# Attention work in pairs: scores and a quarter of M issued one behind the other, over four PSUM banks, from the third batch on

## The chip, the cores and the metric

One Trainium2 chip, one of its cores. The metric is the device time of one execution in microseconds (us), the median of three runs. TensorE is PE in the profile, with its weight loads apart as PEld; VectorE is DVE, ScalarE is ACT, SyncE, which issues all DMAs here, is SP.

## The reference

```python
def sm_attn(qq, kk, vv):                       # 8 batches, 8 heads, 576 tokens, head size 64
    s = scale * np.matmul(qq, kk.transpose(0, 1, 3, 2))
    s = s - np.max(s, axis=-1, keepdims=True)
    a = np.exp(s)
    a = a / (np.sum(a, axis=-1, keepdims=True) + 1e-09)
    return np.matmul(a, vv)
p_packed = sm_attn(p, k, v)                    # 32 landmarks p per head
out = sm_attn(q, p_packed, p_packed)
x = out as (4608, 512)
h = np.maximum(x @ w_in, 0.0); x = h * h @ w_out            # first MLP, 2048 wide
h = x @ w_in2; g = h / (1.0 + np.exp(-1.702 * h)); g @ w_out2   # second MLP, 2048 wide
```

All in fp32.

## The kernel before

**Stages.** The first half of the span holds the attention and the first MLP, the second half the second MLP (`mm_a`, `mm_b`), which the change leaves alone. In the first part the work goes by *slots*: one slot is one chunk of 128 of the 2048 hidden columns for one half (288 tokens) of one batch. Slots 0 to 63 serve batches 0 and 1; from then on every batch has 32 slots, two halves of 16. A slot issues on PE six matmuls `h` (`mm1`, recorded at L112, the helper `prod`) and twelve matmuls `y` (`mm2`, L524). ACT takes `h` out of PSUM with a relu (L493) and squares it (L503; three chunks of 16 are squared on DVE, L501), ACT and DVE split the square into two parts (L202, L204), and `y` reads these. `h` runs three slots ahead of `y` (`LA = 3`, L37).

**Attention beside it.** x is never formed with `w_in`: M = (second softmax's values) times `w_in` is built in four quarters of 512 columns (`m_step`, L450 to L472), and `h` multiplies M by the softmax weights `a`. The attention of batch b runs in the 32 slots of batch b-1, at slots that the list `steps` (L874 to L877) gives, counted from s0 = 32(b-1): scores of the landmarks with k, one half of the tokens each (`s1`, L309) at 0 and 1; their exponentials (`s1b`) at 4; transposes and products with v (`tr`, `pv`, `t2`) at 7 to 10; scores of q, one half each (`s2a`, L394) at 12 and 17, with their softmax (`s2b`) at 16 and 20 and split (`s2c`) at 17 and 26; the quarters of M (`m_step`) at 19, 21, 26 and 29.

**PE's part of these.** `s1`, `s2a` and `m_step` all issue 16 small fp32 matmuls through `heads` (L299 to L307): for each of eight heads, 64 rows by 32 columns of the array, so that the eight occupy it side by side, and each in two instructions. The other work on PE uses the full 128 by 128 array. Two result tiles take two PSUM banks.

**PSUM.** Eight banks: four for `y` (`acc`), two for `h` (`mm_p`), two for attention (`at_p`). `att_tile` (L294) gives an attention tile a bank of `at_p`, and one of `mm_p` only in batch 0. Results leave so: M by two ACT copies (L468) and two DVE subtractions (L470), q scores by two DVE transposes (L401), landmark scores of the first half by a DVE maximum (L319) and an ACT copy (L323) each, of the second half by a maximum and, at `s1b`, the exponentials (L338).

**Order.** Every engine runs its own queue in program order. One pass of the loop at L1000 issues the splits of the slot two ahead, the `h` of the slot three ahead, the `y` of its own slot, and then what `plan[s]` lists, step by step in turn (`interleave`, L811). Conversions of the second MLP's weights (L145 to L155, L230 to L251) are listed in the same plan, about two every eight slots of those whose number modulo 16 is 1 to 13 (`CALM`).

**Loads.** A quarter of M reads two tiles of `w_in` (`load_win`, 512 KB each), through three buffers. They are issued at slot 9 (three; for batch 2 at 14) and then two, two and one at the slots of the first, second and third quarter (`ws`, L884 to L889); each waits until the quarter that used the buffer has been computed. All DMAs go through SP's one queue.

Of the kernel before, what the change touches and what calls it, by code (L numbers as in the profile page):

```python
# [8 lines left out]
F32 = mybir.dt.float32  # L9
# [13 lines left out]
P = 128  # L23
# [52 lines left out]
def fused_kernel(ctx, tc, qT, kT, vv, pT, w_in, w_out, w_in2, w_out2, out):  # L76
# [217 lines left out]
    def att_tile(b, alt, name):  # L294

        pool, tag = (mm_p, "mm") if b == 0 and alt else (at_p, "at")
        return pool.tile([P, 512], F32, tag=tag, name=name)
# [11 lines left out]
    def s1(b, hf):  # L309
        c = slice(hf * HS, (hf + 1) * HS)  # L310
        ps = [att_tile(b, hf, f"s1_{b}_{hf}_{r}") for r in range(2)]
# [35 lines left out]
    def tr(b, r):  # L347
# [6 lines left out]
        pa_ = att_tile(b, r, f"tr_{b}_{r}_a")  # L354
        pb_ = att_tile(b, r, f"tr_{b}_{r}_b")
# [14 lines left out]
    def pv(b, r):  # L370
        t = e1T.pop((b, r))
        v = vt.pop((b, r))
        ps = att_tile(b, r, f"pv_{b}_{r}")
        for c in range(5):
            n = P if c < 4 else 64
            for hp in range(4):
                nc.tensor.matmul(ps[32 * hp:32 * hp + 32, :D], t[:n, c, 32 * hp:32 * hp + 32], v[:n, c, hp * D:(hp + 1) * D],  # L377
                                 start=c == 0, stop=c == 4)
        yield 1
        if r == 0:  # L380
            pp[b] = pp_p.tile([P, 2, D], F32, tag="ppb", name=f"ppb{b}", bufs=1)
        nc.vector.tensor_scalar(out=pp[b][:, r, :], in0=ps[:, :D], scalar1=rs[b][:, 5, r:r + 1], scalar2=None, op0=ALU.mult)
# [11 lines left out]
    def s2a(b, hf):  # L394
        ps = [att_tile(b, hf == 0, f"s2_{b}_{hf}_{r}") for r in range(2)]
# [54 lines left out]
    def m_step(b, f):  # L450
        w = [wt.pop((b, f, g)) for g in range(2)]
        if (b, f) == (0, 0):
            ps = [acc_p.tile([P, 512], F32, tag=f"acc{r}", name=f"m_{b}_{f}_{r}") for r in range(2)]
        else:
            ps = [at_p.tile([P, 512], F32, tag="at", name=f"m_{b}_{f}_{r}") for r in range(2)]
# [406 lines left out]

    for b in range(1, B):
# [7 lines left out]
        else:  # L871
            s0 = (b - 1) * 2 * NFC
            at_k, at_v, at_q, at_w = -5, -2, (2, 3, 5, 6), 9
            steps = [(0, s1, 0), (1, s1, 1), (4, s1b), (7, tr, 0), (8, pv, 0), (8, tr, 1), (9, pv, 1),  # L874
                     (10, t2), (12, s2a, 0), (16, s2b, 0), (17, s2c, 0), (17, s2a, 1), (20, s2b, 1), (26, s2c, 1)]

            steps += [(s, m_step, f) for f, s in enumerate((19, 21, 26, 29))]  # L877
# [3 lines left out]
        if b > 1:  # L881
            for s, f, *a in steps:
                at(s0 + s, f, b, *a)
# [116 lines left out]
    for s in range(done("y"), len(slots)):  # L1000
# [9 lines left out]
        drain(second, s)  # L1010
# [32 lines left out]
```

## Time and profile before

| | before |
|---|---|
| three runs | 1433.84 us median, 1433.5 to 1436.06 |
| the profiled execution | 1436.79 us |
| its span | 1434.9 us |
| PE busy | 1412.7 us (98%) |
| ACT busy, DVE busy | 835.8 us (58%), 951.2 us (66%) |
| granted TensorE clock, mean | 0.999 |

The span is what the profiler saw from the first to the last instruction. A busy time counts an engine as busy while any instruction is in flight; matmuls are pipelined, so that a plain slot's six and twelve matmuls last 295 ns and more each but follow each other much more closely. What a group of matmuls costs is therefore read from the start of the group to the start of the next.

### The profile page before, as it was taken

To read this page: it belongs to the slowest core of one execution; us is meant where nothing else is said; L and a number is where in the kernel's file an instruction comes from. 1 tells how busy PE (TensorE), PEld (TensorE's weight loads), DVE (VectorE), ACT (ScalarE), POOL (GpSimd) and SP (SyncE) were. 2 spreads that over 40 slices of the span, in tenths; PEclk is the share of its full clock that TensorE was granted. 3 is DMA by queue.
4 is the path that set the end of the run, shared out by engine and by line. 5 is a ranking of instruction groups with operands and counts; after the bars stand their busy time and mean duration, and the time that the engine had idled before them with its cause. 6 is when DMAs were issued, how large, how long until landed. Compare 5 with 4: busy or idle time off the path is not lost.

```text
span 1434.9 us, 24896 instructions
## 1 busy us (share of the span) xinstructions
PE 1412.7 (98%) x9734; PEld 1262.1 (88%) x9734; DVE 951.2 (66%) x1623; ACT 835.8 (58%) x1740; POOL 0.7 (0%) x6
## 2 busy tenths in 40 slices
PE   6999999999999999999999999999999999999999
PEld 4688989889898998999998888888888888999998
DVE  6896475756757657573255778577855875677585
ACT  5878676676776677765564544454444534544452
POOL 0000000000000000000000000000000000000000
PEclk9999999999999999999999999999999999999999
DMA  9848467576664756541325566656665676688675
GB/s 327 288 148 307 162 207 227 176 235 212 200 229 176 251 182 221 186 149 33 125 99 206 205 244 221 217 206 227 227 227 205 220 250 229 248 300 286 253 293 180
DMA packets 110934, 307.95 MB, mean 215 GB/s; under 512 B 9056, under 2 KB 52192, under 8 KB 96736
## 3 DMA queue, kind: packets, MB, share of 16 engines
q1 hardware_dynamic: 110816, 306.35, 62.1%
q8 instruction: 77, 1.26, 0.4%
q14 instruction: 41, 0.34, 0.1%
HBM read 250.94 MB, written 55.38 MB: 213 GB/s over the span
## 4 chain that ended last, share of the span: by engine, by line
PE 93%; DMA 3%; ACT 3%; DVE 1%; issue 0%; SPq 0%; DVEq 0%; ACTq 0%
PE h L112 37%; PE y L524 27%; PE o L112 24%; PE m L307 2%; PE s L307 1%; PE pv L377 1%; DMA wA<-w_d 1%; PE tr_a L357 1%; DMA win<-win_d 0%; DMA raw_wo<-in_w_out 0%; PE h L486 0%; DMA w_d<-wc 0%; DMA p<-in_pT 0%; PE warm L830 0%; ACT e L338 0%; ACT gh L202 0%
## 5 line engine op out<-in xcount | busy, mean ns | idle before, releaser
L524 PE MATMUL y<-gh,wo 128*128 128x288 f32 x2976 | 434.2, 295 | 0.4 <-ACT gh L202 0.2
L524 PEld LDWEIGHTS y<-gh,wo 128*128 128x128 f32 x2976 | 406.2, 188 | 4.4 <-ACT gh L202 1.3
L112 PE MATMUL h<-y,wA 128*128 128x512 f32 (+1 forms) x1680 | 349.8, 367 | 1.4 <-DMA wA<-w_d 1.4
L112 PE MATMUL o<-g,wB 128*128 128x512 f32 (+1 forms) x1680 | 349.0, 367 | 0.0
L112 PEld LDWEIGHTS h<-y,wA 128*128 128x128 f32 x1680 | 305.6, 188 | 42.1 <-issue 2.0
L112 PEld LDWEIGHTS o<-g,wB 128*128 128x128 f32 x1680 | 305.6, 188 | 39.6 <-DMA wB<-w_d 0.4
L112 PE MATMUL h<-a,M 128*128 128x288 f32 x1488 | 242.8, 299 | 1.3 <-ACT r L493 1.3
L112 PEld LDWEIGHTS h<-a,M 128*128 128x128 f32 x1488 | 207.7, 188 | 37.0 <-issue 27.7
L636 ACT ACTIVATE g<-hid 128x1024 fp32r<-128x1024 f32 (+1 forms) x140 | 132.8, 971 | 131.9 <-DVE hid L631 102.3
L204 DVE TENSOR_TENSOR gh<-gf,gh 128x288 fp32r<-128x288 f32 x248 | 111.6, 452 | 121.4 <-ACT gh L202 121.1
L612 DVE TENSOR_TENSOR g<-hid,g 128x1024 fp32r<-128x1024 f32 (+1 forms) x140 | 152.6, 1113 | 42.3 <-ACT g L636 40.7
L493 ACT ACTIVATE r<-h 128x288 f32<-128x288 f32 x256 | 104.1, 407 | 84.2 <-PE h L112 81.0
L700 ACT ACTIVATE r<-h 128x512 f32<-128x512 f32 (+1 forms) x120 | 66.6, 555 | 118.3 <-PE h L112 116.1
L708 DVE TENSOR_TENSOR hid<-h,r 128x512 f32<-128x512 f32 (+1 forms) x120 | 76.0, 634 | 81.7 <-PE h L112 65.3
L202 ACT ACTIVATE gh<-gf 128x288 fp32r<-128x288 f32 x248 | 108.6, 438 | 5.2 <-DVE gf L501 2.7
L718 DVE TENSOR_TENSOR hid<-hid,sg 128x512 f32<-128x512 f32 (+1 forms) x120 | 75.7, 631 | 47.1 <-ACT sg L714 47.0
L503 ACT ACTIVATE gf<-r 128x288 f32<-128x288 f32 x212 | 94.3, 445 | 6.6
L714 ACT ACTIVATE sg<-hid 128x512 f32<-128x512 f32 (+1 forms) x120 | 70.2, 585 | 30.5 <-DVE hid L708 30.3
L470 DVE TENSOR_TENSOR M<-m,M 128x512 fp32r<-128x512 f32 x62 | 41.9, 688 | 45.9 <-ACT M L468 45.2
L631 DVE TENSOR_TENSOR hid<-hid 128x1024 f32<-128x1024 f32 (+1 forms) x60 | 66.1, 1111 | 0.0
L468 ACT ACTIVATE M<-m 128x512 fp32r<-128x512 f32 x62 | 36.0, 593 | 39.8 <-PE m L307 39.7
L714 ACT ACTIVATE sg<-h 128x512 f32<-128x512 f32 (+1 forms) x40 | 22.3, 557 | 32.7 <-PE h L112 32.7
(110 smaller groups left out, 974.5 us busy)
## 6 DMA issues: line engine op xcount, KB each, us to landing
wB<-w_d SPq DMA_DIRECT2D x70, 1024.0 KB, 5.0
wA<-w_d SPq DMA_DIRECT2D x40, 1024.0 KB, 4.9
wA<-w_d SPq DMA_DIRECT2D x40, 768.0 KB, 6.2
win<-win_d SPq DMA_DIRECT2D x56, 512.0 KB, 5.1
w_d<-wc SPq DMA_DIRECT2D x112, 256.0 KB, 3.4
k<-in_kT SPq DMA_DIRECT2D x32, 288.0 KB, 5.4
y_d<-ysb SPq DMA_DIRECT2D x16, 576.0 KB, 3.8
v<-in_vv SPq DMA_DIRECT2D x16, 512.0 KB, 7.0
```

The source lines that it names most:

```text
L112: nc.tensor.matmul(ps, w, x, start=start and i == 0, stop=stop and i == n - 1, skip_group_check=more)
L202: nc.scalar.activation(hi, x, AF.Copy)
L204: nc.vector.tensor_tensor(out=lo, in0=x, in1=hi.bitcast(F32), op=ALU.subtract)
L493: nc.scalar.activation(r, ps[:, :HS], AF.Relu)
L503: nc.scalar.activation(g, r, AF.Square)
L524: nc.tensor.matmul(accs[d][:, :HS], w[:, d * P:(d + 1) * P], t[:, x_, :], start=first, stop=fc == seg[1] and d not in {o[0] for o in ops[n ...
L612: nc.vector.tensor_tensor(out=t[:, :, 1, :n], in0=src, in1=t[:, :, 0, :n].bitcast(F32), op=ALU.subtract)
L636: nc.scalar.activation(t[:, :, 0, :PAIRS[p]], gop[p, i, g, "src"], AF.Copy)
L700: nc.scalar.activation(t[:, 0, :n], bank[p, c, "1"][:, :n], AF.Copy)
L708: nc.vector.tensor_tensor(out=hid(p, c, blk), in0=bank[p, c, b][:, :n], in1=part[p, c, r][:, 0, :n], op=ALU.add)
L714: nc.scalar.activation(t, bank[p, c, "1"][:, :n] if blk == 2 else hid(p, c, blk), AF.Sigmoid, scale=GELU)
L718: nc.vector.tensor_tensor(out=hid(p, c, blk), in0=bank[p, c, "1"][:, :n] if blk == 2 else hid(p, c, blk), in1=part.pop((p, c, "sg", blk)), ...
```

## The change

`att_tile` now goes by its flag alone, and more tiles take the `mm_p` banks: both halves of the q scores from batch 2 on, the first half of the landmark scores from batch 3 on, and the last quarter of M for batches 2 to 6. The list of steps changes from batch 2 on: each half of the q scores (now at 17 and 22) is followed in the same slot by a quarter of M (the first and the second). The third and fourth quarter of batches 2 to 6 move to slots 32 and 34, which are slots 0 and 2 of the next batch's attention, beside that batch's two halves of the landmark scores (whose second half moves from 1 to 2, and `s1b` from 4 to 5). Batch 7 keeps its last two quarters at 26 and 29. In the slot behind such a joint slot, `y` is issued ahead of the splits and the `h`. These are 12 pairs with q scores (batches 2 to 7) and 10 with landmark scores (batches 3 to 7, beside M of batches 2 to 6).

```diff
@@ -293,7 +293,7 @@
 
     def att_tile(b, alt, name):
 
-        pool, tag = (mm_p, "mm") if b == 0 and alt else (at_p, "at")
+        pool, tag = (mm_p, "mm") if alt else (at_p, "at")
         return pool.tile([P, 512], F32, tag=tag, name=name)
 
     def heads(ps, w, x):
@@ -308,7 +308,7 @@
 
     def s1(b, hf):
         c = slice(hf * HS, (hf + 1) * HS)
-        ps = [att_tile(b, hf, f"s1_{b}_{hf}_{r}") for r in range(2)]
+        ps = [att_tile(b, hf == (0 if b > 2 else 1) and b != 1 and b != 2, f"s1_{b}_{hf}_{r}") for r in range(2)]
         heads(ps, lambda hp: pt[b][:, hp, :], lambda hp: kt[b, hp][:, c])
         if hf == 0:
             rs[b] = st_p.tile([P, 6, 2], F32, tag="st", name=f"st{b}")
@@ -351,8 +351,8 @@
         else:
             t = e1t_p.tile([P, 5 * P], F32, tag="e1t", name=f"e1t_{b}_{r}")
         t = e1T[b, r] = t.rearrange("p (c k) -> p c k", c=5)
-        pa_ = att_tile(b, r, f"tr_{b}_{r}_a")
-        pb_ = att_tile(b, r, f"tr_{b}_{r}_b")
+        pa_ = att_tile(b, b == 0 and r, f"tr_{b}_{r}_a")
+        pb_ = att_tile(b, b == 0 and r, f"tr_{b}_{r}_b")
         for c in range(4):
             nc.tensor.transpose(pa_[:, c * P:(c + 1) * P], e[:, c * P:(c + 1) * P], ident)
         nc.tensor.transpose(pb_[:64, :P], e[:, 512:576], ident)
@@ -370,7 +370,7 @@
     def pv(b, r):
         t = e1T.pop((b, r))
         v = vt.pop((b, r))
-        ps = att_tile(b, r, f"pv_{b}_{r}")
+        ps = att_tile(b, b == 0 and r, f"pv_{b}_{r}")
         for c in range(5):
             n = P if c < 4 else 64
             for hp in range(4):
@@ -392,7 +392,7 @@
     NB = HS // 32
 
     def s2a(b, hf):
-        ps = [att_tile(b, hf == 0, f"s2_{b}_{hf}_{r}") for r in range(2)]
+        ps = [att_tile(b, b > 1 or b == 0 and hf == 0, f"s2_{b}_{hf}_{r}") for r in range(2)]
         heads(ps, lambda hp: ppT[b][:, 32 * hp:32 * hp + 32], lambda hp: qt[b, hp][:, hf * HS:(hf + 1) * HS])
         yield 1
         t = s2_p.tile([P, 2 * NB, 32], F32, tag="s2t", name=f"s2t{b}_{hf}", bufs=1)
@@ -452,7 +452,7 @@
         if (b, f) == (0, 0):
             ps = [acc_p.tile([P, 512], F32, tag=f"acc{r}", name=f"m_{b}_{f}_{r}") for r in range(2)]
         else:
-            ps = [at_p.tile([P, 512], F32, tag="at", name=f"m_{b}_{f}_{r}") for r in range(2)]
+            ps = [att_tile(b, 1 < b < B - 1 and f == 3, f"m_{b}_{f}_{r}") for r in range(2)]
         heads(ps, lambda hp: ppT[b][:, 32 * hp:32 * hp + 32], lambda hp: w[hp // 2][:, hp % 2, :])
         yield 1
         if b == 0 and 4 * f < NFULL:
@@ -860,6 +860,7 @@
         g = running[k] if k in running and name != "warm" else macros[name](*map(int, a))
         running[k] = None if g is None or next(g, running) is running else g
 
+    joint = set()
     for b in range(1, B):
         if b == 1:
             s0 = 0
@@ -871,16 +872,17 @@
         else:
             s0 = (b - 1) * 2 * NFC
             at_k, at_v, at_q, at_w = -5, -2, (2, 3, 5, 6), 9
-            steps = [(0, s1, 0), (1, s1, 1), (4, s1b), (7, tr, 0), (8, pv, 0), (8, tr, 1), (9, pv, 1),
-                     (10, t2), (12, s2a, 0), (16, s2b, 0), (17, s2c, 0), (17, s2a, 1), (20, s2b, 1), (26, s2c, 1)]
-
-            steps += [(s, m_step, f) for f, s in enumerate((19, 21, 26, 29))]
+            s1s = [(0, s1, 0), (1, s1, 1), (4, s1b)] if b == 2 else [(0, s1, 0), (2, s1, 1), (5, s1b)]
+            steps = s1s + [(7, tr, 0), (8, pv, 0), (8, tr, 1), (9, pv, 1), (10, t2), (17, s2a, 0), (17, m_step, 0), (19, s2b, 0),
+                           (21, s2c, 0), (22, s2a, 1), (22, m_step, 1), (25, s2b, 1), (27, s2c, 1)]
+            steps += [(s, m_step, f) for f, s in ((2, 32), (3, 34))] if b < B - 1 else [(26, m_step, 2), (29, m_step, 3)]
+            joint |= {s0 + s for s, f, *a in steps if f is m_step and b < B - 1 or f is s2a}
         ld = loads(b)
         for n, (f, *a) in enumerate(ld):
             at(s0 + (at_k if n < 5 else at_v if n < 7 else at_q[n - 7]), f, *a)
         if b > 1:
             for s, f, *a in steps:
-                at(s0 + s, f, b, *a)
+                (plan[s0 + s].insert(0, (f, (b, *a))) if f is s1 and a == [0] else at(s0 + s, f, b, *a))
         ws = [s for s, f, *_ in steps if f is m_step]
         if b == 2:
             at_w = 14
@@ -997,7 +999,9 @@
     nfirst, nsplit = done("f"), done("g")
     for _ in range(4):
         ahead()
-    for s in range(done("y"), len(slots)):
+
+    def lead(s):
+        nonlocal nfirst, nsplit
         while nsplit < min(s + LA, nfirst):
             drain(parts, nsplit)
             nsplit += 1
@@ -1007,7 +1011,14 @@
         while nsplit <= s:
             drain(parts, nsplit)
             nsplit += 1
-        drain(second, s)
+
+    for s in range(done("y"), len(slots)):
+        if s - 1 in joint and nsplit > s:
+            drain(second, s)
+            lead(s)
+        else:
+            lead(s)
+            drain(second, s)
         interleave(plan[s])
         for _ in range(plan_end[s]):
             ahead()
```

## Rows read from the trace of the kernel before

**Rows 1.** The page: the granted clock in 40 slices.
```profile
PEclk9999999999999999999999999999999999999999
```

**Rows 2.** Windows: length; busy PE, PEld, DVE, ACT, POOL; clock; DMA share; GB/s.
```profile
437.00:513.00 76.00, 76.00 (x642) 69.23 (x641) 51.52 (x117) 54.18 (x141) 0.00 (x0) 1.00 0.60 202
```

**Rows 3.** Timeline of PE, 440 to 460 us: start, time to last end, what.
```profile
448.25 0.95 PE L112 MATMUL h<-a,M 128*128 128x288 f32 x6
449.04 1.74 PE L524 MATMUL y<-gh,wo 128*128 128x288 f32 x12
450.71 0.72 PE L307 MATMUL s<-q,ppT 64*32 64x288 f32 x16
451.36 1.06 PE L112 MATMUL h<-a,M 128*128 128x288 f32 x6
452.25 1.75 PE L524 MATMUL y<-gh,wo 128*128 128x288 f32 x12
...
454.62 1.74 PE L524 MATMUL y<-gh,wo 128*128 128x288 f32 x12
456.30 1.09 PE L307 MATMUL m<-win,ppT 64*32 64x512 f32 x16
457.32 1.06 PE L112 MATMUL h<-a,M 128*128 128x288 f32 x6
458.21 1.75 PE L524 MATMUL y<-gh,wo 128*128 128x288 f32 x12
```

**Rows 4.** Timeline of PE from 19.10 us, cut at 19.40, 19.66 and 19.905.
```profile
19.15 0.48 PE L307 MATMUL s<-q,ppT 64*32 64x288 f32 x8 [0.30 <-ACT ppT L389]
...
19.15 0.91 PE L307 MATMUL s<-q,ppT 64*32 64x288 f32 x17 [0.30 <-ACT ppT L389]
...
19.15 1.15 PE L307 MATMUL s<-q,ppT 64*32 64x288 f32 x23 [0.30 <-ACT ppT L389]
```

**Rows 5.** Timeline, all engines, 276 to 290 us: M's first two quarters, batch 3.
```profile
279.05 1.09 PE L307 MATMUL m<-win,ppT 64*32 64x512 f32 x16
...
280.18 0.88 SPq L290 DMA_DIRECT2D win<-win_d  x2
...
285.01 1.06 PE L307 MATMUL m<-win,ppT 64*32 64x512 f32 x8
...
287.38 1.06 PE L307 MATMUL m<-win,ppT 64*32 64x512 f32 x8 [1.30 <-DMA win<-win_d]
...
288.37 1.06 PE L112 MATMUL h<-a,M 128*128 128x288 f32 x6
```

**Rows 6.** The chain, 455 to 466 us: start, time to the next piece, what.
```profile
462.33 1.40 PE m L307 x16
```

**Rows 7.** L290, the loads of w_in for M, over the whole span.
```profile
DMA to landing us min/median/max: 3.6/5.1/8.1
```

**Rows 8.** Windows, as in rows 2: the stretch that begins with slot 160.
```profile
492.00:494.00 2.00, 2.00 (x27) 1.37 (x26) 1.01 (x3) 0.25 (x1) 0.00 (x0) 1.00 1.01 324
```

**Rows 9.** Timeline, 485 to 489 us: behind a quarter of M (ended at 485.11).
```profile
485.11 1.06 PE L112 MATMUL h<-a,M 128*128 128x288 f32 x6
...
485.27 0.60 ACT L468 ACTIVATE M<-m 128x512 fp32r<-128x512 f32 x1 [1.76 <-PE m L307]
...
487.19 0.58 ACT L468 ACTIVATE M<-m 128x512 fp32r<-128x512 f32 x1
...
487.81 0.69 DVE L470 TENSOR_TENSOR M<-m,M 128x512 fp32r<-128x512 f32 x1 [0.62 <-ACT M L468]
488.01 0.40 ACT L493 ACTIVATE r<-h 128x288 f32<-128x288 f32 x1
```

**Rows 10.** Timeline of ACT, 497 to 503 us: the relu in a slot without attention work.
```profile
499.75 0.41 ACT L493 ACTIVATE r<-h 128x288 f32<-128x288 f32 x1 [0.84 <-PE h L112]
```

**Rows 11.** Timeline of PEld from 19.10 us, cut at 19.41 and 19.42.
```profile
19.14 0.18 PEld L307 LDWEIGHTS s<-q,ppT 64*32 64x32 f32 x16 [0.54 <-ACT ppT L389]
...
19.14 0.38 PEld L307 LDWEIGHTS s<-q,ppT 64*32 64x32 f32 x17 [0.54 <-ACT ppT L389]
```

## The prediction

> **What bounds the kernel now.** The first view is the page: PE is busy 98% of the span and its clock is granted in full in every slice [rows 1], so the clock is no term here. The change touches slots 32 to 223, about a third of the span, and the second view, windows over such a stretch, tells what limits them: in 76 us PE is never idle, ACT is busy 54.18 us and DVE 51.52 us [rows 2]. PE's queue sets the pace, and ACT and DVE have some 30% to spare. A microsecond off PE's queue there is a microsecond off the end, as long as nothing new makes PE wait.
>
> The third view, PE's timeline, tells what a slot costs. Read it from start to start, as the durations overlap. A slot without attention work takes 2.37 us from its `y` to the next (452.25 to 454.62). A slot with a half of the q scores takes 3.21 us (449.04 to 452.25), one with a quarter of M 3.59 us (454.62 to 458.21) [rows 3]. So the half costs **0.84 us** and the quarter **1.22 us**, 2.06 us together. From its first matmul to the `h` behind it the half takes 0.65 us and the quarter 1.02 us [rows 3]; the other 0.19 or 0.20 us is paid at the two edges, where PE goes over to the 64 by 32 arrangement and back.
>
> The fourth view shows two such groups back to back, the first q scores of batch 0. The 16 matmuls of a group start in two sets of eight, and all 32 in four. Cutting the timeline at later and later times shows when each set starts: eight matmuls have started by 19.40, the seventeenth (the second group's first) by 19.66, 0.51 us after the first at 19.15, and the fourth set by 19.905, 0.75 us after [rows 4]. Sets follow each other every 0.24 to 0.26 us across the border of the groups as inside them. There is no edge between two groups of one arrangement.
>
> **The change part by part.** *Pairs.* There are 22. In a pair the scores cost 0.51 us until the quarter's first set can start [rows 4], the quarter 1.02 us as before [rows 3], the outer edges 0.19 us once: 1.72 us where 2.06 us stood. That saves 0.34 us per pair, **7.5 us** in all. Bounds: nothing, if a group should pay its edges wherever it stands, and 0.36 us (0.84 less the two sets' 0.48), 7.9 us in all. I take 0.34, as the back-to-back scores are the same instructions. Less than nothing is excluded for this term, since PE issues the same 32 matmuls; waits are terms of their own.
>
> A rule of the Trainium skill speaks against it (TensorE: Matmul & The Clock Gate, section The mechanism): a weight load overlaps running matmuls only where its row group differs. By it the quarter's loads, which go to the same row groups as the scores, would wait for these; it returns as a rival below.
>
> *The second quarter's loads.* Today the second `w_in` pair is asked for when the first quarter is done and is needed two slots later. In batch 3 the load goes out at 280.18, the quarter starts at 285.01, waits in its middle and ends at 288.37, 3.36 us in place of 1.02: 2.34 us lost [rows 3, 5]. In batch 5 it takes 1.40 us, 0.38 lost [rows 6]. The other second quarters lose nothing. With the first quarter at 17 and the second at 22 the distance is five slots, so **2.7 us** go in this execution (bounds: 0 if the same load is late again, and 2.7).
>
> *The fourth quarter's loads.* The same arrangement comes back here: in batches 2 to 6 the last tile waits until the third quarter, at slot 32, has used its buffer, and the fourth needs it at 34 (26 and 29 before). The load goes out 1.13 us after its quarter starts (279.05 to 280.18) [rows 5], so 1.64 us into the pair. The fourth quarter starts 1.72 us and two plain slots, 4.74 us, after the pair's start, at 6.46. That leaves 4.8 us, and landings take 3.6 to 8.1 us, 5.1 in the median [rows 7]. The last store of the half and the next loads are beside it; the stretch behind the slot of one batch has the DMA engines full [rows 8]. Bounds: 0 and 5 times 3.3 us, 16.5. I take the mean of the six second quarters, whose lead was the same (2.72 over 6, 0.45 us): **2.3 us** lost over five. On SP the next batch's q loads, stores and raw loads stand behind this waiting load; the q are wanted five slots later than now (17, not 12), so that costs nothing unless SP is held beyond those.
>
> *The banks.* A pair needs four, two of them `h`'s. Two waits can come of it. **Before the pair:** both `h` banks must have gone through the relu. The last `h` ends at 449.20 and a group starts at 450.71, a slack of 1.51 us [rows 3]. In a slot without attention work ACT is waiting for `h`, and the relu takes 0.41 us [rows 10]. Only behind a quarter's copies was it late: `h` ended at 486.17, the relu at 488.41, 2.24 us later [rows 9], 0.73 us beyond the slack. In the new list no quarter stands in the slots just before a pair but for 32 ahead of 34, with a whole slot between. I take nothing for the 17 pairs with q scores or a first half of landmark scores, with 0.73 each (12.4 us) as their bound. **Behind the pair:** `y` goes first now and covers the emptying, then two `h` come in a row, the second 2.37 us after the pair's end, 4.09 us after its start. Scores leave by one DVE operation per bank. The fourth quarter needs two copies and two subtractions: its last subtraction ended at 488.50, 3.39 us after the quarter's end at 485.11 [rows 9], while the second `h` comes 4.09 less 1.02, 3.07 us, after it. That is 0.32 us late, with weight conversions between the copies, as in those rows. Bounds for the five: 0 and 1.6 us; I take **1.0 us**, since such conversions stand in some of the slots only.
>
> *What moves at no cost.* The scores' softmax and the first two quarters finish well ahead of the slots that read them, hidden by the `y` and `h` of at least five slots. The third and fourth quarters are first read by `h` of the next batch's chunks 8 and 12, issued at slots 37 and 41 counted as here: five and seven slots of cover. `s1b` comes a slot later, two before the transposes that read it; without that cover each late slot would cost up to 2.37 us.
>
> **The sum.** 7.5 and 2.7 gained, 2.3 and 1.0 lost: 6.9 us off the profiled execution's 1436.79, 1429.9. That execution stands 2.95 us above the median of 1433.84, and the 2.34 us wait of batch 3 is of that size; where the median's run has no such wait, its gain is 4.6 us, 1429.2, and where it has it, 1426.9. I give **1427.5**.
>
> **The rivals.** *The fourth quarter starves (slower).* If its load lands at 8.1 us in all five batches [rows 7], 16.5 us are lost in place of 2.3, against 10.2 gained, and with the banks' 1.0 the time is 1433.84 + 7.3 = 1441.1. It decides from 10.2 less 1.0 over 5, 1.84 us of wait, a landing of 6.6 us. For: the landing lies beyond the lead in the median, and the engines are full once [rows 8]. Against: the tiles now come alone, not in twos as at 280.18 [rows 5], and four of six with this lead arrived in time.
>
> *The banks give the gain back.* If the relus are late as behind a quarter today [rows 9], 0.34 us each is enough to eat the pairs, and 1433 remains. For: ACT is busy 71% of this stretch [rows 2] and its queue is strict. Against: it waits for `h` in the plain slots [rows 10].
>
> *The weights are not loaded ahead.* If the third and fourth set each wait for their loads, some 0.11 us (the seventeenth load starts after 19.41 and ends at 19.52), a pair saves 0.12 us, 2.6 us in all in place of 7.5, and the time is 1432.4. Against: that load was over 0.14 us before its matmul at 19.66, while the second set was running [rows 4, 11]. By the skill's rule it should not have been; on this row the trace does not agree.
>
> *The change does not make pairs.* Should the quarter's own banks or tiles arrive later than the scores, PE stands between them and nothing but the earlier loads is gained: 1433.
>
> **The numbers.** A measurement of this kernel can tell about 0.2%, 2.9 us, from no change. The forecast, 1424 to 1430, has 0.62; better than that (all pairs at the bound and no fourth quarter late) 0.05; the banks 0.14, a part of it still over 0.2%; starving 0.09; the weights 0.05; no pairs 0.05. So faster 0.75, the same 0.17, slower 0.08. The range, 1423 to 1433, reaches from the best sum to the cases that give the gain back, and leaves starving out.
>
> **What would show it.** In the profile after, 32 small matmuls stand in one piece, some 1.53 us from their start to the next `y`; second quarters take 1.02 us; fourth quarters show what waits on `w_in` remain; releasers of `h` and of the pairs name relu, transposes or M's subtractions if the banks bind. PE's plain slots stay at 2.37 us. The forecast is wrong if a pair's cost is near 2.06 us, or if idle time of PE between slots 32 and 223 adds up to more than 5 us.

## The result and the profile after

The changed kernel is **slower**: 1446.46 us in the median of six runs (1442.32 to 1449.71), beside 1436.21 (1433.5 to 1437.15) for the kernel before; the ratio is 1.0074, its 95% interval 1.0052 to 1.0096. Measured again beside later experiments it was 1448.24, ratio 1.0076 (1.0055 to 1.0096). The forecast was 1427.5, with 1433 as its upper end; it started from 1433.84, and 2.4 us of the distance are only the kernel before, whose six runs have the higher median. The profiled execution took 1445.9 us, its span is 1444.1.

From the page of the changed kernel, two lines: the granted clock, which answers to [rows 1] and is still full in every slice, and the engines' shares of the chain that ended last (93% PE and 3% DMA before).

```profile
PEclk9999999999999999999999999999999999999999
...
PE 83%; DMA 7%; ACT 5%; DVE 3%; issue 1%; SPq 0%; ACTq 0%; DVEq 0%
```

The clock is no part of the story. The chain is another matter: PE's share falls by a tenth of the span, and DMA, ACT and DVE take it. Windows over the stretch of [rows 2] say the same of PE:

```profile
437.00:513.00 76.00, 71.42 (x594) 64.05 (x593) 46.51 (x105) 48.26 (x123) 0.00 (x0) 1.00 0.57 192
```

PE is idle for 4.58 of 76 us, where it was never idle before. From 160 to 700 us it is 10.6 us idle, and 1.5 before. ACT and DVE are less busy than before, so neither has become the bound.

**The pairs work.** PE's timeline of the changed kernel, a pair of batch 4 with nothing late (start, time to the last end, what), then that batch's second quarter; these answer to [rows 3] and [rows 5]:

```profile
363.86 1.74 PE L524 MATMUL y<-gh,wo 128*128 128x288 f32 x12
365.53 0.72 PE L307 MATMUL s<-q,ppT 64*32 64x288 f32 x16
366.04 1.06 PE L307 MATMUL m<-win,ppT 64*32 64x512 f32 x16
367.04 1.85 PE L524 MATMUL y<-gh,wo 128*128 128x288 f32 x12
368.72 1.75 PE L112 MATMUL h<-a,M 128*128 128x288 f32 x12
370.31 0.95 PE L524 MATMUL y<-gh,wo 128*128 128x288 f32 x6
```

```profile
379.12 0.71 PE L307 MATMUL s<-q,ppT 64*32 64x288 f32 x16
379.62 1.06 PE L307 MATMUL m<-win,ppT 64*32 64x512 f32 x16
380.62 1.85 PE L524 MATMUL y<-gh,wo 128*128 128x288 f32 x12
```

From start to start the scores take 0.51 us (365.53 to 366.04), the quarter 1.00, and `y` stands 0.10 us longer behind them; with the edge ahead of the scores this is some 1.70 us where 2.06 stood. The second quarter finds its tiles there: 1.00 us, no gap.

**The chain from 200 to 740 us** tells what takes the time. The line sums the chain by what it runs through, first of the kernel before, then of the changed one:

```profile
by line: PE y L524 57.2%; PE h L112 29.6%; PE m L307 4.1%; PE s L307 2.4%; PE pv L377 1.5%; DMA win<-win_d 1.3%; DMA w_d<-wc 1.1%; PE tr_a L357 0.9%; issue 0.3%; ACT gh L202 0.2%; PE tr_b L358 0.2%; ACT M L468 0.2%; ACT gf L503 0.2%; ACT wc
```

```profile
by line: PE y L524 42.8%; PE h L112 21.6%; DMA w_d<-wc 7.0%; PE m L307 3.9%; DMA win<-win_d 2.7%; PE s L307 2.3%; issue 1.8%; PE pv L377 1.5%; ACT gh L202 1.4%; ACT r L493 1.2%; DVE M L470 1.2%; DMA k<-in_kT 1.2%; PE tr_a L357 0.9%; ACT gf 
```

The piece that has grown is `DMA w_d<-wc`, from 1.1% of 540 us to 7.0%, from some 6 us to 38. It is no load of the attention and no bank: it is the store of a converted weight tile of the second MLP. Each such tile is written by a copy on ACT (line 241) and a subtraction on DVE (line 246) one slot later, is stored by SP (lines 249, 251), and there are three tiles, so the copy three tiles on waits until the store has landed.

How that reaches PE can be followed in batch 5. SP's queue, the chain, ACT's and PE's timelines of the changed kernel, behind the pair of 467.47:

```profile
469.11 0.33 SPq L173 DMA_DIRECT2D raw_p<-in_w_out  x1
469.80 1.29 SPq L290 DMA_DIRECT2D win<-win_d  x2
471.20 3.03 SPq L251 DMA_DIRECT2D w_d<-wc  x2
```

```profile
470.78 0.42 ACT M L468
471.20 8.69 DMA w_d<-wc
...
479.98 0.10 ACT wc L241
...
480.30 0.43 ACT gh L202
480.73 0.31 ACT r L493
```

```profile
474.26 0.45 ACT L503 ACTIVATE gf<-r 128x288 f32<-128x288 f32 x1
479.98 0.42 ACT L241 ACTIVATE wc<-sum 128x256 fp32r<-128x256 f32 x1 [5.28 <-DMA w_d<-wc]
```

```profile
477.74 1.75 PE L524 MATMUL y<-gh,wo 128*128 128x288 f32 x12
481.08 1.05 PE L112 MATMUL h<-a,M 128*128 128x288 f32 x6 [1.59 <-ACT r L493]
```

The step list of the change puts a quarter's end in this slot, and with it two `w_in` loads (469.80). The stores come behind them, and the first (471.20) takes 8.69 us to land. ACT reaches the copy that needs the tile after 474.7 and stands there for 5.28 us. The relu is queued behind that copy, so `h` has no free bank, and PE stands idle for 1.59 us at 481.08, over 11 us after the pair ended. ACT has such waits of 3 us and more five times in the changed kernel (3.73 to 5.28 us) and once in the kernel before. Behind each of the five, within 4 us of its end, PE waits too, 7.0 us in all.

The stores as a whole did not become slower: 30 of the 112 take over 5 us to land in the changed kernel and 32 in the one before, the longest 8.69 and 8.24. In both kernels each of these was asked for while a load ahead of it was still under way; with none under way a store took 2.05 us in the median after and 2.02 before. What changed is which stores are late and what stands behind the wait for them: the store that takes 8.69 us here took 4.38 in the kernel before.

**That one wait before, and its likeness after**, show why the same wait can cost nothing. ACT and PE of the kernel before, then of the changed one, both beside batch 6:

```profile
522.44 0.45 ACT L503 ACTIVATE gf<-r 128x288 f32<-128x288 f32 x1
527.80 0.42 ACT L241 ACTIVATE wc<-sum 128x256 fp32r<-128x256 f32 x1 [4.91 <-DMA w_d<-wc]
...
528.45 0.39 ACT L493 ACTIVATE r<-h 128x288 f32<-128x288 f32 x1
```

```profile
523.38 0.95 PE L112 MATMUL h<-a,M 128*128 128x288 f32 x6
...
525.84 0.72 PE L307 MATMUL s<-q,ppT 64*32 64x288 f32 x16
...
528.96 0.99 PE L112 MATMUL h<-a,M 128*128 128x288 f32 x6
```

```profile
532.65 0.45 ACT L503 ACTIVATE gf<-r 128x288 f32<-128x288 f32 x1
538.00 0.42 ACT L241 ACTIVATE wc<-sum 128x256 fp32r<-128x256 f32 x1 [4.90 <-DMA w_d<-wc]
...
538.65 0.39 ACT L493 ACTIVATE r<-h 128x288 f32<-128x288 f32 x1
```

```profile
533.58 0.95 PE L112 MATMUL h<-a,M 128*128 128x288 f32 x6
...
536.74 1.74 PE L524 MATMUL y<-gh,wo 128*128 128x288 f32 x12
539.10 1.09 PE L112 MATMUL h<-a,M 128*128 128x288 f32 x6 [0.61 <-ACT r L493]
```

ACT stands for 4.91 and 4.90 us. Before, a half of the q scores (525.84) lay between the `h` of 523.38 and the one of 528.96 that needs its bank: 5.58 us, and PE didn't wait. After, that half is with its quarter in a pair elsewhere, the same distance is two plain slots, 4.74 us (twice the 2.37 of [rows 3]), and PE waits (539.10): 5.52 us in all. In this place the score group that stood alone had spaced out the slots, and the pair took that away. That the same holds at the other places is argued from these rows; no run here shows it apart.

**Where the time went**, from PE's timeline: time from start to start beyond what the same group costs undisturbed, from 160 us to the second MLP, comes to 4.4 us before and 21.3 after, 16.9 more. Less the pairs' 7.5 that is 9.4; the same work took 9.2 longer there (a `y` that started 1.0 us later than before at 165.8 us, and the last one 10.3). The 21.3 are: the fourth quarters' own tile, 5.1; the second `h` or the `y` behind a fourth quarter, 3.0; before or inside pairs with q scores, 2.7; behind the pairs of batch 2, 1.0; `k` late, 0.7; and the rest, above all waits far from any pair as in the rows just shown (for a relu, or for ACT's copy of `y`, L538), 8.8.

### The profile page after: what moved, and what is told of

It is laid out like the page before. It is cut to its first block, busy times and chain, and to the rows that moved or that the text cites. A ratio compares the mean times of both kernels' runs of the same rounds, so it can differ in the third digit from the quotient of the medians.

```text
span 1444.1 us, 24947 instructions
## 1 busy us (share of the span) xinstructions
PE 1412.8 (98%) x9734; PEld 1267.0 (88%) x9734; DVE 949.7 (66%) x1623; ACT 833.3 (58%) x1740; POOL 0.7 (0%) x6
## 3 DMA queue, kind: packets, MB, share of 16 engines
q8 instruction: 77, 1.26, 0.4%
## 4 chain that ended last, share of the span: by engine, by line
PE 83%; DMA 7%; ACT 5%; DVE 3%; issue 1%; SPq 0%; ACTq 0%; DVEq 0%
PE h L112 34%; PE o L112 24%; PE y L524 21%; DMA w_d<-wc 3%; PE m L307 2%; PE s L307 1%; DMA win<-win_d 1%; DMA raw_win<-in_w_in 1%; DMA raw_wo<-in_w_out 1%; PE pv L377 1%; DMA k<-in_kT 1%; ACT r L493 1%; ACT gh L202 1%; DVE M L470 1%; DMA wA<-w_d 1%
## 5 line engine op out<-in xcount | busy, mean ns | idle before, releaser
L112 PE MATMUL h<-a,M 128*128 128x288 f32 x1488 | 237.7, 298 | 5.3 <-ACT r L493 5.2
L241 ACT ACTIVATE wc<-sum 128x256 fp32r<-128x256 f32 x64 | 26.0, 407 | 28.5 <-DMA w_d<-wc 27.8
```

What stands on the lines that cost most here:

```text
L112: nc.tensor.matmul(ps, w, x, start=start and i == 0, stop=stop and i == n - 1, skip_group_check=more)
```

## The experiments

PE's waits are counted as just said; the last column is the count, in 200 to 660 us, of ACT's waits of 3 us and more for a store at line 241. Ratios are to the kernel before on the same chip. The changed kernel itself is the row "again"; the kernel before has 4.4 us and 1. PE's waits inside the transposes are left out; they matter in before_pool (2.8 us) and poolstore (1.1). Four edits come out near 1442.3, some 0.3% under the unedited kernel; but for lasttile their intervals touch its own, so what each of them is worth by itself is not settled.

| run | median us | ratio, 95% interval | PE's waits us | ACT 3 us+ |
|---|---|---|---|---|
| calm | 1442.26 | 1.0044 (1.0027 to 1.0060) | 17.6 | 4 |
| qpairs | 1436.42 | 1.0000 (0.9989 to 1.0011) | 8.1 | 2 |
| spairs | 1438.32 | 1.0013 (1.0001 to 1.0026) | 11.4 | 4 |
| lasttile | 1442.16 | 1.0036 (1.0021 to 1.0050) | 15.2 | 5 |
| poolstore | 1442.32 | 1.0042 (1.0028 to 1.0057) | 14.9 | 5 |
| before_pool | 1439.44 | 1.0026 (1.0013 to 1.0038) | 7.1 | 2 |
| spread | 1442.30 | 1.0045 (1.0029 to 1.0060) | 16.3 | 4 |
| fix34 | 1436.35 | 0.9996 (0.9983 to 1.0010) | 13.1 | 6 |
| again | 1448.24 | 1.0076 (1.0055 to 1.0096) | 22.1 | 5 |
| lo_after | 1433.72 | 0.9973 (0.9960 to 0.9987) | 7.0 | 1 |
| lo_fix34 | 1428.10 | 0.9934 (0.9911 to 0.9957) | 3.2 | 0 |
| lo_before | 1438.22 | 1.0003 (0.9987 to 1.0020) | 7.6 | 1 |
| hold_after | 1444.87 | 1.0059 (1.0036 to 1.0082) | 20.4 | 5 |
| late_after | 1448.70 | 1.0100 (1.0073 to 1.0126) | 23.6 | 5 |

**calm: the weight conversions kept out of the slots around pairs.**

```diff
-    calm = [s for s in range(45, SB - 2 * NFC) if s % 16 in CALM]
+    calm = [s for s in range(45, SB - 2 * NFC) if s % 32 not in (0, 2, 3, 17, 18, 22, 23)]
```

> The changed kernel with the weight conversions of the second MLP listed in other slots: away from every pair and the slot behind it (slot numbers 0, 2, 3, 17, 18, 22 and 23 modulo 32), and in slots 14 to 16, 30 and 31 instead. Theory Queues (beside a pair, DVE and ACT have the emptying of four banks, the softmax of a half and a conversion at once; their queues fall behind, conversion tiles and relus come late, and PE stops for an h bank): nearly all waits at the pairs with q scores go, some 13 us, and the time is 1438 us or less. Theory Load (the fourth quarter waits for its w_in): no change, 1446 us. Theory Banks (lending h's banks stops PE whatever else the queues hold): no change, 1445 to 1447 us.

1442.26, between what the theories gave. The waits before the pairs of q scores went, and those at the ends of the halves grew (4.6 us at 397 to 404 alone): moving the conversions moves the wait on a store with them, up to 6.23 us in one piece.

**qpairs and spairs: one kind of pair alone.** The first pairs only the q scores, with the third and fourth quarters and the landmark scores where they were; the second pairs only the landmark scores.

```diff
...
-            steps += [(s, m_step, f) for f, s in ((2, 32), (3, 34))] if b < B - 1 else [(26, m_step, 2), (29, m_step, 3)]
-            joint |= {s0 + s for s, f, *a in steps if f is m_step and b < B - 1 or f is s2a}
+            steps += [(26, m_step, 2), (29, m_step, 3)]
+            joint |= {s0 + s for s, f, *a in steps if f is s2a}
```

```diff
...
-            steps = s1s + [(7, tr, 0), (8, pv, 0), (8, tr, 1), (9, pv, 1), (10, t2), (17, s2a, 0), (17, m_step, 0), (19, s2b, 0),
-                           (21, s2c, 0), (22, s2a, 1), (22, m_step, 1), (25, s2b, 1), (27, s2c, 1)]
+            steps = s1s + [(7, tr, 0), (8, pv, 0), (8, tr, 1), (9, pv, 1), (10, t2), (12, s2a, 0), (16, s2b, 0), (17, s2c, 0),
+                           (17, s2a, 1), (20, s2b, 1), (26, s2c, 1), (19, m_step, 0), (21, m_step, 1)]
...
```

> Only the 12 pairs with q scores; landmark scores, third and fourth quarters and their banks as before the change. Theory Queues: 4.1 us gained in pairs, up to 2.7 in second quarters, about 13 lost in waits: 1441 to 1444 us, slower than before. Theory Load: no loss is left, 1430 to 1433 us. Theory Banks: its share of the loss, 1441 to 1443 us.

> Only the 10 pairs with landmark scores; q scores with the first two quarters at their slots and banks of before the change. Theory Queues: 3.4 us gained, about 8 lost, 5 of these on the fourth quarter's load: 1440 to 1442 us. Theory Load: 1446 us, the whole loss. Theory Banks: 1440 to 1442 us.

1436.42 and 1438.32: no difference from the kernel before, and slightly slower. Both lie outside what any of the three theories gave. Neither kind loses what both together lose (10 to 11 us), so the loss is no fixed price per pair.

**lasttile: the fourth quarter without its late tile.** In batches 2 to 6 the fourth quarter uses its first `w_in` tile twice; the last tile is loaded but left out of M.

```diff
         w = [wt.pop((b, f, g)) for g in range(2)]
+        if f == 3 and 1 < b < B - 1:
+            w[1] = w[0]
```

> The changed kernel, but the fourth quarter of batches 2 to 6 reads its first w_in tile twice in place of its second, so that it doesn't wait for the tile loaded last (which is still loaded, and left unread). Theory Load as the whole cause: 1436 us or less. Theory Queues: only the 5 us that the trace shows at the fourth quarter go, 1441 us. Theory Banks: 1441 us as well, with the waits at the second h behind the fourth quarter (0.2 to 0.8 us) still there.

1442.16. The fourth quarters' wait of 5.1 us goes but for 0.43; of the 10 to 11 us of loss 5.4 stay. Starving, the rival that was to make the change slower, is about half of the loss and not the whole.

**poolstore and before_pool: the stores of the converted tiles on GpSimd's queue**, in the changed kernel and in the one before.

```diff
-            nc.sync.dma_start(out=w1_d[:, 2 * q:2 * q + 2, ORDER_A.index(i), d], in_=o.bitcast(F32))
+            nc.gpsimd.dma_start(out=w1_d[:, 2 * q:2 * q + 2, ORDER_A.index(i), d], in_=o.bitcast(F32))
...
-            nc.sync.dma_start(out=w2_d[:, ORDER_B.index(i), u - 8], in_=o.bitcast(F32))
+            nc.gpsimd.dma_start(out=w2_d[:, ORDER_B.index(i), u - 8], in_=o.bitcast(F32))
```

> The changed kernel with one line moved: the stores of the converted second-MLP weights (L249, L251) are issued on GpSimd's queue, which is idle, in place of SP's. Theory Stores (a conversion tile comes back late because its store stands behind waits and behind w_in, k and v loads on SP's one queue; ACT holds at the next conversion with relus behind it, and PE waits for an h bank): the waits at the ends of the halves and at the q pairs go, some 9 of the trace's 21 us; 1436 to 1439 us. Theory Queues alone (DVE and ACT have too much beside a pair): no change, 1445 to 1447 us. If issuing there is itself slow, slower.

> The kernel before with the same stores on GpSimd's queue: the control. Theory Stores: 0 to 1 us faster, as its trace shows 0.7 us of such waits on PE: 1435 to 1436 us. Any theory under which the other queue is faster for its own sake: as much gained as in the changed kernel.

1442.32 and 1439.44, neither as expected: the changed kernel gains less than the theory of the stores gave it, and the kernel before loses. Another queue doesn't free ACT: its waits for the stores are 32.2 us in the changed kernel, more than with SP. In the kernel before the move costs some 3 us; in the changed one the time is below the unedited kernel's, and so are PE's waits (16.0 us with those in the transposes, against 22.1); why was not settled. The Trainium skill (Trainium Kernel Development and Optimization, section Key Constraints) says that DMAs from SP's and GpSimd's queues run on the same 16 DMA engines and that another queue saves issue time only. The runs agree in so far as the stores land no sooner: on GpSimd's queue 31 of 112 take over 5 us, the longest 8.6, beside 30 and 8.69 on SP's.

**spread: the `w_in` loads one at a time**, at slots 17, 19, 24, 26 and 32, not in twos behind a quarter.

```diff
-            at(s0 + (at_w if n < 3 else ws[(n - 3) // 2]), load_win, b, f, n % 2)
+            at(s0 + (at_w if n < 3 else (17, 19, 24, 26, 32)[n - 3] if b < B - 1 else ws[(n - 3) // 2]), load_win, b, f, n % 2)
```

> The changed kernel with the w_in loads of batches 2 to 6 asked for one at a time (slots 17, 19, 24, 26 and 32 in place of two at 17, two at 22 and one at 32). Theory Stores, with the loads that come in twos as what the stores stand behind: 2 to 5 us faster than the change, 1441 to 1444 us. If it is the waiting on SP and not the volume: no change, 1446 us.

1442.30, as the theory had it, but not by its means: three fourth quarters wait 0.4 to 0.5 us each and the others not at all, while ACT's waits for stores stay, 29.1 us. The loads that come in twos are not all of it.

**fix34: the last pair three slots later** (slot 37, the second half of the landmark scores at 5 in place of 2), with the fourth quarter in banks of its own.

```diff
-        ps = [att_tile(b, hf == (0 if b > 2 else 1) and b != 1 and b != 2, f"s1_{b}_{hf}_{r}") for r in range(2)]
+        ps = [att_tile(b, b > 2 or b == 0 and hf, f"s1_{b}_{hf}_{r}") for r in range(2)]
...
-            if b > 0 and hf == 0:
+            if b > 0 and (hf == 0 or b > 2):
...
-            ps = [att_tile(b, 1 < b < B - 1 and f == 3, f"m_{b}_{f}_{r}") for r in range(2)]
+            ps = [att_tile(b, False, f"m_{b}_{f}_{r}") for r in range(2)]
...
-            s1s = [(0, s1, 0), (1, s1, 1), (4, s1b)] if b == 2 else [(0, s1, 0), (2, s1, 1), (5, s1b)]
+            s1s = [(0, s1, 0), (1, s1, 1), (4, s1b)] if b == 2 else [(0, s1, 0), (5, s1, 1), (8, s1b)]
+            d = 0 if b == 2 else 3
...
-            steps += [(s, m_step, f) for f, s in ((2, 32), (3, 34))] if b < B - 1 else [(26, m_step, 2), (29, m_step, 3)]
+            steps += [(s, m_step, f) for f, s in ((2, 32), (3, 37))] if b < B - 1 else [(26, m_step, 2), (29, m_step, 3)]
```

> The changed kernel with the last pair moved: the second half of the landmark scores and the fourth quarter at slot 5 in place of 2 (from batch 3 on, with what follows up to t2 three slots later and the q loads at 2, 6, 7 and 8), the landmark scores in h's banks and copied out at once, the fourth quarter in the attention's. The load then has five slots and h waits for no subtraction of M. All theories that price the fourth quarter as its trace does (5.1 us for the load, 2.5 to 3 us behind it): 1438 to 1440 us. If holding SP for the later q loads, or ACT's two more copies a batch, cost as much: 1444 us or more.

1436.35, a little below what was expected. Both waits at the fourth quarter are gone, and the time is that of the kernel before, not less: PE's waits are 8.7 us more than before, against the 7.5 of the pairs. In the chain of this kernel from 200 to 740 us `DMA w_d<-wc` has 8.3%: what remains is the stores.

**lo_after, lo_fix34, lo_before: the subtraction and the store late in the slot of the copy**, not in the next, in the changed kernel, in fix34 and in the kernel before; "again" is the changed kernel beside them.

```diff
     def unit_lo(u, i):
+        for _ in range(4):
+            yield
         o, x = wcs.pop((u, i))
...
-                at(j + 1, unit_lo, u - 1, i)
+                at(j, unit_lo, u - 1, i)
```

> The changed kernel once more, unedited, as a control on the same chip as the other kernels of this call. Its runs so far went from 1442.3 to 1449.7 us, and four edits of it that each took away a different wait all came out near 1442.3, so that its own median has to be seen beside them. Both theories expect 1443 to 1447 us, 0.5 to 0.75% over the kernel before; 1442 or less would mean that those four edits were worth nothing.

> The changed kernel, with the second half of each weight conversion (the subtraction and the store) issued late in the slot of its copy, not in the slot after: each tile's store leaves one slot (about 2.4 us) earlier, and ScalarE's copy three tiles on waits that much less for it. Theory (ScalarE stands at its conversion copy until an earlier store has landed, and the relus behind it empty h's banks late): the 27.8 us of ScalarE at line 241 behind that store fall below 12, the 7.7 us far from the pairs below 3.5, the 2.7 us before the pairs of q's scores to about 1.5, and the time falls by 4 to 6 us, to 1439 to 1442. Rival (those waits come from VectorE being late with the reductions and subtractions behind a pair, or from the throttled banks themselves, the store being only last in line): ScalarE's wait at line 241 moves to VectorE's subtraction or disappears, and the time stays within 1.5 us of the unedited one.

> The version with the fourth quarter three slots later (1436.35 us) with the same earlier stores. Its remaining 13 us of TensorE waits are near the pairs of q's scores (2.7 and 1.0) and far from pairs (8.4). Theory of the stores: the 8.4 fall by 5 or more, 1430 to 1432.5 us, 0.25% or more under the kernel before. Rival: the same as without the edit, 1435 to 1437.5 us.

> The kernel before with the same earlier stores, which tells how much of what the edit brings belongs to the change. The kernel before waits only 0.7 us on TensorE far from its score slots, though ScalarE stands for 21.5 us at line 241 behind stores. If the earlier stores only take slack that TensorE doesn't feel there: 1435 to 1437 us, no difference. If they are worth the same there as in the changed kernel: 1431 to 1433.

1448.24 (a little over what was expected), **1433.72**, **1428.10** and 1438.22. The edit takes 14.5 us off the changed kernel, more than twice what the theory expected, and nothing off the kernel before; with it fix34 comes out below what was expected. The median time from the end of a copy to its subtraction falls from 1.78 to 0.40 us, to its store from 2.46 to 1.10, and 15 of the 112 stores take over 5 us in place of 30. ACT's waits for stores (all waits at that line: us, times, longest), in the changed kernel, with the edit, and fix34 with it:

```profile
ACT wc L241 <- DMA w_d<-wc: 27.8, 10, 5.3
```

```profile
ACT wc L241 <- DMA w_d<-wc: 6.4, 5, 3.2
```

```profile
ACT wc L241 <- DMA w_d<-wc: 6.9, 6, 2.4
```

The chain from 200 to 740 us has no `DMA w_d<-wc` left among its larger pieces:

```profile
by line: PE y L526 57.4%; PE h L112 29.2%; PE m L309 3.8%; PE s L309 2.3%; PE pv L379 1.5%; DMA win<-win_d 1.2%; PE tr_a L359 0.9%; DVE M L472 0.4%; DVE s2t L407 0.3%; DVE s2st L405 0.2%; issue 0.2%; ACT M L470 0.2%; PE tr_b L360 0.2%; ACT 
```

In the stretch of batch 5 shown above, SP and ACT now go like this:

```profile
458.89 3.36 SPq L253 DMA_DIRECT2D w_d<-wc  x2
462.30 1.21 SPq L173 DMA_DIRECT2D raw_p<-in_w_out  x1
463.60 0.86 SPq L292 DMA_DIRECT2D win<-win_d  x2
```

```profile
467.41 0.40 ACT L241 ACTIVATE wc<-sum 128x256 fp32r<-128x256 f32 x1
...
471.12 0.42 ACT L241 ACTIVATE wc<-sum 128x256 fp32r<-128x256 f32 x1 [1.26 <-DMA w_d<-wc]
```

The two stores of the row of 458.89 stand ahead of the two `w_in` loads (463.60). The second of them, issued at 461.93, is the one that took 8.69 us behind the loads, and takes 2.69 here. The copy that waited 5.28 us for it (now at 467.41) doesn't wait, the next one waits 1.26 us, and PE's waits from 477 to 486 us have no counterpart. The waits at the fourth quarters shrink too, from 5.1 to 2.2 us: the 14.5 are more than the far waits and the q scores' 11.5 together.

**hold_after and late_after** tell apart what the edit moved: the store, and the place of the subtraction in DVE's order. The first keeps the early subtraction and lets the store wait for two columns that DVE subtracts again in the next slot; the second keeps the late place in the slot, but of the next slot.

```diff
     def unit_lo(u, i):
+        for _ in range(4):
+            yield
+        o, x = wcs[u, i]
+        nc.vector.tensor_tensor(out=o[:, :, 1, :], in0=x, in1=o[:, :, 0, :].bitcast(F32), op=ALU.subtract)
+
+    def unit_st(u, i):
         o, x = wcs.pop((u, i))
-        nc.vector.tensor_tensor(out=o[:, :, 1, :], in0=x, in1=o[:, :, 0, :].bitcast(F32), op=ALU.subtract)
+        nc.vector.tensor_tensor(out=o[:, :, 1, :1], in0=x[:, :, :1], in1=o[:, :, 0, :1].bitcast(F32), op=ALU.subtract)
...
-                at(j + 1, unit_lo, u - 1, i)
+                at(j, unit_lo, u - 1, i)
+                at(j + 1, unit_st, u - 1, i)
```

```diff
     def unit_lo(u, i):
+        for _ in range(4):
+            yield
```

> The changed kernel with the subtraction of each weight conversion early (late in the slot of its copy, where it brought the time from 1448.2 to 1433.7 us), but the tile's store held back to where it was: at the start of the next slot VectorE subtracts two of the tile's columns once more, and the store waits for that. It adds 112 tiny VectorE instructions. Theory (the landing of the store is what ScalarE's copy three tiles on waits for): ScalarE's waits at line 241 behind the store come back to 20 us or more, and so does the time, to 1443 to 1449 us. Rival (the place of the subtraction in VectorE's order is what counts: at the start of a slot it stands ahead of the emptying of banks and of h's split, late in the slot it doesn't): 1433 to 1437 us, the waits behind the store notwithstanding.

> The changed kernel with subtraction and store in the slot after the copy, as they were, but late in it: VectorE's order as in the fast version, the stores another part of a slot later than in the unedited kernel. Theory of the landing: ScalarE's waits at line 241 behind the store grow over 28 us and the time over 1448, to 1450 to 1456 us. Rival (VectorE's order): 1433 to 1440 us.

1444.87 and 1448.70. ACT's waits for the stores, of hold_after and of late_after:

```profile
ACT wc L241 <- DMA w_d<-wc: 28.2, 10, 4.6
```

```profile
ACT wc L241 <- DMA w_d<-wc: 34.9, 17, 5.8
```

With the subtraction as early as in lo_after (0.43 us after the copy in the median) and the store held back (2.55 us after it), the waits are back (28.2 us) and so is most of the time, 1444.87. With the order of DVE as in lo_after and the stores later still (3.38 us after the copy), ACT waits 34.9 us and the time is 1448.70, just under what was expected. The store decides, not DVE's order. hold_after lies 3.4 us under the unedited kernel's 1448.24, measured on another chip, and the two ratios' intervals overlap; what of that is the subtraction's place was not settled. Nor was it settled how much of the loss is the stores' place behind the loads on SP and how much the time lost in itself. late_after speaks for the second: 19 of its stores take over 5 us, near lo_after's 15, and yet the loss is whole. More tiles than three were not tried.

## Why the prediction was wrong

*Pairs, 7.5 us gained:* right. Undisturbed they cost 1.70 us against the 1.72 of the sum, and with the earlier stores there is a gain: lo_after is 4.5 us under lo_before, fix34 with the same edit 10.1. That is not the pairs alone: in lo_before's trace batch 3's second quarter loses 4.9 us to its loads, which the new list of steps avoids. The rival that the weights are not loaded ahead falls with it: the quarter's first set starts 0.51 us after the scores' first (365.53 to 366.04), as within one group. The rival without pairs falls by the same rows. The Trainium skill (TensorE: Matmul & The Clock Gate, section The mechanism) lets a weight load overlap running matmuls only where its row group differs; on this border the trace doesn't agree, as the quarter's first weights are loaded from 365.80 to 365.95, while the scores' second set runs on the same row groups from 365.80 to 366.25.

*The second quarter's loads, 2.7 gained:* right, no second quarter waits for its tiles in the changed kernel.

*The fourth quarter's loads, 2.3 lost:* right in place, at half the measured size. It was 5.1 us: 0.41 and 1.14 of waits in two batches, and 3.56 in batch 5, whose rows on PE and on SP are:

```profile
503.55 1.06 PE L307 MATMUL m<-win,ppT 64*32 64x512 f32 x8
507.14 0.63 PE L307 MATMUL m<-win,ppT 64*32 64x512 f32 x4 [2.52 <-DMA win<-win_d]
```

```profile
493.81 0.49 SPq L281 DMA_DIRECT2D v<-in_vv  x1
...
497.79 0.57 SPq L539 DMA_DIRECT2D y_d<-ysb  x1
498.45 0.80 SPq L290 DMA_DIRECT2D win<-win_d  x1
```

The load goes out at 498.45 behind four pieces of `v`, a store and the output of a half, and lands 8.6 us later (landings of line 290 are 3.4 to 8.6 us here, 5.0 in the median, where [rows 7] has 5.1). With the earlier stores it was 2.2 us; that this is the forecast's size may be luck, as its 2.3 came from a mean over six in which one wait was nearly the whole.

*The banks behind a fourth quarter, 1.0 lost:* the mechanism is right and was well sized, but a second one joined it, and the sum is 3.0 us. In three of the five the second `h` waits for M's second subtraction, and the two `h` take 0.25 us longer each time, where the working had 0.32. In the other two they take 0.85 longer, with these rows behind the fourth quarter of 323.67, which answer to [rows 9]:

```profile
327.34 1.02 PE L112 MATMUL h<-a,M 128*128 128x288 f32 x6
...
327.81 0.69 DVE L470 TENSOR_TENSOR M<-m,M 128x512 fp32r<-128x512 f32 x1
328.40 0.41 ACT L493 ACTIVATE r<-h 128x288 f32<-128x288 f32 x1 [1.44 <-PE h L112]
...
328.86 1.06 PE L112 MATMUL h<-a,M 128*128 128x288 f32 x6 [0.50 <-ACT r L493]
```

The subtraction is through at 328.50, yet the second `h` (328.86) waits for ACT's relu (328.40 to 328.81), which empties the first `h`, of 327.34: from that wait, the two were given one bank; the `h` after them (331.34) waits for no relu, so it has the other freed bank. That was not in the working, nor the 0.1 to 0.3 us that `y` loses in three of these slots.

*Before the pair, nothing:* 2.7 us, all in pairs with q scores (1.9 of it behind one of ACT's five long waits) and down to 1.0 in lo_after.

*"What moves at no cost"* is **the step that failed**: what the moved steps do to the stores was put at nothing, and issuing the stores earlier was worth 14.5 us (1448.24 to 1433.72), more than the whole loss. The prediction named the stores once, in its paragraph on the fourth quarter's loads, as standing behind a waiting load on SP, and priced that at nothing "unless SP is held beyond those". It took only the attention's own tiles as the cover to ask about. The 112 stores of converted weights stand on the same queue, a late one holds one of three tiles, ACT's queue stops at the next copy into it, and the relu is behind that copy. The kernel before showed this chain at work, ACT waiting 21.5 us for such stores in 15 pieces, with PE feeling hardly any of it; the prediction never read that row:

```profile
ACT wc L241 <- DMA w_d<-wc: 21.5, 15, 4.9
```

The changed kernel has only 6.3 us more of it in total, in 10 pieces and not 15. The length of one piece and what stands behind it tell more than the sum: one of more than 3 us before, five after. The number of such pieces alone does not give the time either; fix34 has six. So "ACT and DVE have some 30% to spare" was a true average that priced nothing, and what the prediction itself set as its test, PE idle over 5 us in this stretch, is what happened (10.6 us).

*The rivals.* Starving had the right sign, with 1441.1, by a mechanism that explains 5.1 of the 16.9 us. Banks giving the gain back came nearest in place (the relu is what PE waits for), but named ACT's copies and not what ACT itself waits for. None had the stores.

## What to carry to other kernels

When steps are regrouped, follow every queue to the buffers that its other customers recycle: list who waits for whom on each engine in the profile before, also where it costs nothing today, and ask for the longest single waits as well as the sum. Work that stands alone in a slot is also slack for everything that is a little late, so packing it can cost more than it saves until the slack is put back. Here one early store, worth nothing in the kernel before, turned the same packing from 0.76% slower to 0.27% faster, and with the last pair three slots later to 0.66% faster than the kernel before (0.43 to 0.89%).

## What the runs showed of the hardware

A store of a converted tile lands in 3.0 us in the median of the changed kernel and in 3.4 of the one before, but took 8.69 us behind two loads of `w_in` (471.20). In the changed kernel the median is 2.05 us, and the longest 3.85, where no load asked for earlier is under way, and 4.3 where one is. And stores on GpSimd's queue in place of SP's, nothing else changed, made the kernel before 0.26% slower (0.13 to 0.38%) and ACT's waits for them longer, 28.1 us in place of 21.5.
